# Two scatters pulled forward, four query loads moved to other buffers, and a DRAIN ahead of each store

## The chip, the cores and the metric

The kernel runs on one core of one Trainium2 chip. A core has five instruction queues that work at the same time: PE (matmuls), DVE (elementwise on vectors), ACT (activations), POOL (GpSimd) and SP (here it only issues DMAs). PE's weight loads are listed apart as PEld. The metric is the device time of one execution in microseconds (us), median of several runs.

## The reference, cut to what matters

Two stages follow each other. A linear attention gives 4608 rows of 512 numbers, and a mixture of experts sends each row through the one expert that its direction fits best:

```python
def phi(x):
    proj = np.einsum('bhsd,md->bhsm', x, omega)
    h = proj - np.sum(x * x, axis=-1, keepdims=True) / 2.0
    return np.exp(h - np.max(h, axis=-1, keepdims=True)) / np.sqrt(m)
q_p, k_p = phi(q * scale), phi(k * scale)
kv = np.einsum('bhsm,bhsd->bhmd', k_p, v)
out = einsum(q_p, kv) / (einsum(q_p, k_p.sum(2)) + 1e-6)      # 8 x 576 rows of 8 heads x 64
...
expert_idx = np.argmax(xn @ en.T / tau, axis=1)               # one of 8 experts for each row
for e in range(E):
    mask = expert_idx == e
    h = np.maximum(x[mask] @ w1[e], 0.0)                      # 512 -> 1024
    out[mask] = gate_w[mask, None] * (h @ w2[e])              # 1024 -> 512
```

## The kernel before, in words

**First stage: 36 tiles of 128 rows.** Queries and keys come as 36 tiles each. A loop over i (L711) handles key tile i and query tile iq = i - 7 together, so that i runs from 0 to 44: up to i = 6 there are only keys, from i = 36 on only queries. For a query tile the order on PE is: its projection (L362, 16 small matmuls), the transposes of the tile before (L449, 16), and the product with the finished key-value sums (L469, 32). ACT makes the exponentials (L375) and copies half of the transposes (L454), DVE makes the maxima (L366), the other copy (L456) and the normalised row tile xr (L482 to L488).

**Routing.** After each third query tile a generator (routed, L493) picks the experts of the three tiles, works out the place of each row in a table in memory (xs), sorted by expert, and POOL then writes each of the three tiles there with one indirect DMA, a scatter (L555). The generator is cut into nine steps. A list named plan (L837 to L844) says after which part of which iteration each step runs: (ends, k) is the end of iteration k, (mid, k, n) and (spare, k, n) are slots inside it. The last three steps are the three scatters. Three tiles are a group; there are 12, numbered from 0, so that the ninth is group 8, tiles 24 to 26, and its plan is made at i = 34. POOL runs its instructions in the order in which they are written.

**Queries and keys.** Each query tile (qt) goes through a ring of two buffers, as each key tile (kt) does through another. SP issues the load of query tile iq + 2 at the top of iteration i (loadq, L349; called at L713); a load waits until PE has done the projection that last read its buffer. The last key tile, 35, is read by PE in iteration 35. SP takes its loads in order: a load that waits holds those behind it.

**Beside the last iterations** the kernel already loads the weights of the most frequent expert (rf, L584), splits them into a high and a low part (L590 to L599; the low part on POOL), and starts on that expert's first two tiles of rows (first_steps, fs_x, fs_a, fs_o in the rows), among them a square root in 13 small POOL instructions (root, L138; rtt_p, rt_p in the rows).

**Second stage: 38 steps of 128 rows.** In each step PE does 24 matmuls with w1 (pb, L278) and 24 with w2 (po, L278); each takes 512 columns. POOL makes the low parts of the next weights in four pieces for w1 and four for w2 (L233) and between them stores the finished rows of an earlier step into the output with an indirect DMA (store, L307 to L315). The steps 0 and 1 are the two early tiles, the rest runs from t = 2 to 37; a further loop for more steps is not entered with these inputs.

Of the kernel before, what the change touches and what calls it, by code (L numbers as in the profile page):

```python
# [11 lines left out]
F32 = mybir.dt.float32  # L12
# [10 lines left out]
P = 128  # L23
# [6 lines left out]
NTILE = NSB * TPS  # L30
# [9 lines left out]
NPRE = 2  # L40
# [2 lines left out]
FILLS = {36: 1, 37: 1, 38: 1, 39: 1, 40: 1, 41: 1, 42: 1, 43: 2, 44: 4}  # L43
PADP = 8
ONACT = 5
PIECE = 256
SHIFTW = 16
BESIDE = 32
# [13 lines left out]
def attention_moe(ctx: ExitStack, tc: tile.TileContext, qT, kT, v1, omT, emb, tau, w1q, w2q, xs, out):  # L62
    nc = tc.nc
# [155 lines left out]
    def wsplit(wn, t, raw, dv, dp):  # L219
# [7 lines left out]
        else:  # L227
            ih = nc.vector.tensor_copy(at(h, dv), raw)  # L228
            ils = []
            piece = F if t is None or t >= NSTAT - 2 else PIECE  # L230
            for c in range(0, F, piece):
# [73 lines left out]
        return gp.tile([P, n], F32, name=f"{name}{t}", tag=name, bufs=2)  # L305

    def store(t, xg):  # L307
        w = nc.gpsimd.indirect_dma_start(
            out=out, out_offset=bass.IndirectOffsetOnAxis(ap=xg[:, PAY - 1 : PAY].bitcast(I32), axis=0),
            in_=xg[:, 0:DM], in_offset=None, bounds_check=N - 1, oob_is_err=False,  # L310
        )
        for o in outs:
            tc.declare_no_dep(w.ins, o.ins.name, reason="other tokens")
        outs.append(w)

    with ExitStack() as c1:
        p1 = c1.enter_context(tc.tile_pool(name="p1", bufs=2))
# [4 lines left out]
        kva, kvs, st = {}, {}, {}  # L322
# [25 lines left out]

        def loadq(i):  # L349
            if 0 <= i < NTILE:  # L350
                st["q", i] = p1.tile([P, 4, P], F32, name=f"qt{i}", tag="qt", bufs=2)
                nc.sync.dma_start(st["q", i], qT[i])


# [231 lines left out]
        def first_split(n):  # L586
            q, (_, h, l) = n // 2, W[("w1", "w2")[n % 2]]
            raw = st["rf", n]
            if n % 2 == 0 or n >= ONACT:
                nc.scalar.activation(h[:, 0, q, :], raw, AF.Copy)  # L590
# [10 lines left out]
        def first_steps():  # L601
# [16 lines left out]
            def down(t, cs, po):  # L618
                for c in cs:
                    computed("w2", t, products(po, pre_h[t], "w2", 0, [c], 0, c == 0, c == 7))  # L620
                    yield
                if c == 7:
                    scaled(po, xgp[t], total[:, t : t + 1])
                    store(t, xgp[t])
# [68 lines left out]
        early, spare, mid, ends, behind = {}, {}, {}, {}, []  # L693
# [16 lines left out]
        loop.enter_context(tc.manual_schedule(engines={ET.DVE, ET.Activation}))  # L710
        for i in range(NTILE + LAG + 2):  # L711
            iq = i - LAG
            loadq(iq + 2)  # L713
            ahead = i + (4 if i < 2 else 2)
            if i < 2 or i >= 4:
                load(ahead)
# [116 lines left out]
            if sums and done % G == G - 1:  # L833
                g = done // G
                steps = routed(g)
                if g == GPICK:
                    plan = [(ends, i), (mid, i + 1, 2), (mid, i + 1, 1), (spare, i + 2, 0), (mid, i + 2, 0)]  # L837
                    plan += [(mid, i + 3, 2), (mid, i + 3, 1)] + [(ends, i + 3 + k) for k in range(3)]
                elif i >= NTILE:
                    plan = [(ends, i)] * 3 + [(spare, i + 1, 0), (mid, i + 1, 0), (mid, i + 1, 1)]  # L840
                    plan += [(ends, i + 1 + k) for k in range(3)]
                else:
                    plan = [(ends, i), (mid, i + 1, 2), (mid, i + 1, 1), (spare, i + 2, 0), (mid, i + 2, 0)]
                    plan += [(mid, i + 3, 2)] + [(ends, i + 3 + k) for k in range(3)]  # L844
                for d, *key in plan:
                    (at(d, *key) if key[0] < NTILE + LAG + 2 else behind).append((next, steps, None))
            go(ends, i)
# [10 lines left out]
            if i in LOADS:  # L858
                n = LOADS.index(i)
# [16 lines left out]
        t = lambda n, w=E, dt=F32: once.tile([P, w], dt, name=n)  # L876
# [164 lines left out]
    with tc.manual_schedule(engines={ET.PE, ET.Activation, ET.DVE, ET.Pool, ET.SP}):  # L1041
        xt[NPRE] = pre_x[0]
        turn, ends = {}, NSTAT - 1
# [70 lines left out]
        for t in range(NPRE, NSTAT):  # L1114
# [15 lines left out]
            def ended():  # L1130

                for v in list(po):
                    scaled(po.pop(v), xg[v], gates[v])
                    store(v, xg[v])
# [13 lines left out]
            if t > SHIFT:  # L1148
                for v in list(po):
                    po.pop(v)  # L1150
                    store(v, xg[v])
                split("w2", u)
                if t == ends:
                    split("w1", t)
# [153 lines left out]
```

## Time and profile before

| | us |
|---|---|
| median of 3 runs (lowest, highest) | 659.11 (658.09, 659.37) |
| the profiled execution | 658.08 |
| its span, first to last instruction | 656.5 |
| PE busy | 629.6 |
| DVE busy | 496.5 |
| ACT busy | 430.8 |
| POOL busy | 424.7 |

A busy time is the time in which at least one instruction of that engine runs; the ends of matmuls are modelled. Times in the rows count from the start of the span. A row of a timeline is: start, duration, engine, line, operation, what is written and read, how many, and in brackets how long the engine had been idle and what ended that. "issue" stands where nothing that the profile shows was waited for, "remote" where what released the engine could not be found.

### The profile page before, as it was taken

What the parts mean: (1) busy time and instruction counts of PE and PEld (TensorE: products, weight loads), DVE (VectorE), ACT (ScalarE), POOL (GpSimd) and SP (SyncE); (2) the same over time, 40 slices, a digit from 0 to 9 for tenths busy, and PEclk for the clock granted to TensorE, in tenths of its full rate; (3) what the DMA queues carried; (4) which work ended last, traced back from release to release, by engine and by line L of the source; (5) the groups of instructions that cost most, each with busy time, mean ns of one, the idle gap of its engine ahead of it and who ended that gap; (6) DMA issues with size and microseconds to landing.
All of it is one profiled execution on the core that took longest, in us unless ns stands there. A gap on an engine that the chain in (4) does not pass through costs nothing.

```text
span 656.5 us, 19022 instructions
## 1 busy us (share of the span) xinstructions
PE 629.6 (96%) x6289; PEld 534.6 (81%) x6290; DVE 496.5 (76%) x926; ACT 430.8 (66%) x1102; POOL 424.7 (65%) x585
## 2 busy tenths in 40 slices
PE   9999999999998899999999999999999999999992
PEld 8899898889876788888888888888888888888871
DVE  5788888898978654686778786868787867787940
ACT  6899888888895425655666665666565656666420
POOL 2113343335986234668879797888878886798862
PEclk9999999999999999999999999999999999999996
DMA  7546666667943168859778788888787977787620
GB/s 263 182 149 194 191 193 206 196 198 267 327 139 131 50 195 306 258 148 251 211 223 212 222 212 224 211 221 222 203 232 210 244 200 196 224 219 214 172 85 35
DMA packets 142238, 131.92 MB, mean 201 GB/s; under 512 B 106742, under 2 KB 106870, under 8 KB 142144
## 3 DMA queue, kind: packets, MB, share of 16 engines
q1 hardware_dynamic: 135520, 109.70, 59.2%
q0 software_dynamic: 6480, 20.91, 9.1%
q8 instruction: 57, 0.93, 0.6%
q14 instruction: 37, 0.30, 0.1%
q10 hardware_dynamic: 144, 0.07, 0.0%
HBM read 83.78 MB, written 21.97 MB: 161 GB/s over the span
## 4 chain that ended last, share of the span: by engine, by line
PE 84%; ACT 5%; DVE 4%; issue 2%; POOL 2%; DMA 1%; SPq 0%; POOLq 0%; DVEq 0%; ACTq 0%
PE pb L278 30%; PE po L278 29%; PE pb L362 8%; PE nuu L469 4%; PE kva L393 4%; ACT ftq L375 2%; PE nuu L449 2%; ACT ftk L375 2%; PE fs_o L278 2%; PE fs_a L278 1%; PE nuu L393 1%; PE pb L260 1%; PE nuu L431 1%; DVE xr L488 1%; ACT qp L454 1%
## 5 line engine op out<-in xcount | busy, mean ns | idle before, releaser
L233 POOL TENSOR_TENSOR w1l<-raww,w1h 128x256 f32 (+1 forms) x130 | 123.2, 947 | 44.7 <-DVE w1h L228 37.1
L233 POOL TENSOR_TENSOR w2l<-raww,w2h 128x256 f32 (+1 forms) x130 | 144.2, 1110 | 11.9 <-DVE w2h L228 3.5
L278 PE MATMUL po<-w2h,hh 128*128 (+1 forms) x288 | 112.3, 390 | 0.4 <-POOL w2l L233 0.4
L278 PE MATMUL po<-w2h,hl 128*128 (+1 forms) x288 | 112.2, 390 | 0.0
L278 PE MATMUL po<-w2l,hh 128*128 (+1 forms) x288 | 112.1, 389 | 0.0
L278 PE MATMUL pb<-w1h,xh 128*128 (+1 forms) x280 | 109.5, 391 | 0.0
L278 PE MATMUL pb<-w1h,xl 128*128 (+1 forms) x280 | 109.3, 390 | 0.0
L278 PE MATMUL pb<-w1l,xh 128*128 (+1 forms) x280 | 109.0, 389 | 0.0
L1031 DVE COPY pl<-pb 128x512 uint16<-128x512 uint16 x68 | 46.7, 689 | 60.4 <-ACT pl L1027 60.3
L375 ACT ACTIVATE ftk<-pb,nmk 128x128 f32<-128x128 f32 x288 | 80.5, 457 | 4.9 <-DVE nmk L366 4.9
L375 ACT ACTIVATE ftq<-pb,nmq 128x128 f32<-128x128 f32 x288 | 80.4, 417 | 2.0 <-DVE nmq L366 1.3
L1027 ACT ACTIVATE pl<-pb 128x512 uint16<-128x512 uint16 x68 | 39.3, 582 | 60.3 <-DMA t<-pl 42.5
L1049 DVE COPY wd<-t 128x1024 uint16<-128x1024 uint16 x68 | 67.1, 989 | 1.3 <-DMA t<-pl 1.2
L1065 ACT ACTIVATE hh<-wd 128x1024 fp32r<-128x1024 f32 x34 | 36.1, 1063 | 46.9 <-DVE wd L1049 41.3
L278 PEld LDWEIGHTS po<-w2h,hh 128*128 128x128 f32 x288 | 54.0, 188 | 11.9 <-POOL w2l L233 0.8
L278 PEld LDWEIGHTS po<-w2h,hl 128*128 128x128 f32 x288 | 54.1, 188 | 11.5 <-DVE hl L1069 0.4
L278 PEld LDWEIGHTS po<-w2l,hh 128*128 128x128 f32 x288 | 54.1, 188 | 11.3
L278 PEld LDWEIGHTS pb<-w1h,xl 128*128 128x128 f32 x280 | 52.5, 188 | 11.6 <-DVE xl L1068 0.6
L278 PEld LDWEIGHTS pb<-w1l,xh 128*128 128x128 f32 x280 | 52.6, 188 | 10.8
L278 PEld LDWEIGHTS pb<-w1h,xh 128*128 128x128 f32 x280 | 52.6, 188 | 10.7
L1069 DVE SCALAR_TENSOR_TENSOR hl<-wd,hh 128x1024 fp32r<-128x1024 f32 x34 | 53.7, 1580 | 7.2 <-ACT hh L1065 6.8
L366 DVE TENSOR_REDUCE nmq<-pb 128x4 f32<-128x512 f32 x72 | 48.6, 683 | 7.3 <-PE pb L362 6.0
(333 smaller groups left out, 1229.4 us busy)
## 6 DMA issues: line engine op xcount, KB each, us to landing
raww<-w1q SPq DMA_DIRECT2D x38, 512.0 KB
raww<-w2q SPq DMA_DIRECT2D x38, 512.0 KB
kt<-kT SPq DMA_DIRECT2D x36, 256.0 KB
qt<-qT SPq DMA_DIRECT2D x36, 256.0 KB
xgp<-xs SPq DMA_DIRECT2D x20, 260.5 KB
xg<-xs SPq DMA_DIRECT2D x18, 260.5 KB
rf<-w1q SPq DMA_DIRECT2D x4, 512.0 KB
rf<-w2q SPq DMA_DIRECT2D x4, 512.0 KB
```

Source lines behind the costliest of these rows:

```text
L233: ils.append(nc.gpsimd.tensor_tensor(at(l, dp)[:, c], raw[:, c], at(h, dp)[:, c].bitcast(F32), op=ALU.subtract))
L278: done.append(nc.tensor.matmul(dst, x[:, c * P : (c + 1) * P], ws.rearrange("p o f -> p (o f)"), start=(begin and i == 0 and k == 0), stop ...
L362: nc.tensor.matmul(st["pj" + w, i, a][:, c, :], st[w, i][r, c, :], om[r, :], start=True, stop=True)
L366: nc.vector.tensor_reduce(nm, st["pj" + which, i, a], axis=AX.X, op=ALU.max, negate=True)
L375: nc.scalar.activation(ft[:, h, :], pj[:, h, :], AF.Exp, bias=nm[:, h : h + 1])
L393: nc.tensor.matmul(acc[c : c + 64, h, :], ft[:, h, c : c + 64], vt[:, 2 * h + a, :], start=begin and h == 0, stop=u == 4 + 4 * b and h == 3,)
L469: nc.tensor.matmul(pn[a][s * D : s * D + D, h, :], st["qp", i, s][:, 2 * h + a, :], kvs[sb, int(u > 4 - s)][:, 4 * a + h, :], start=True, ...
L1027: nc.scalar.activation(planes[1][:, o : o + 512], halved(src)[:, :, 1], AF.Copy)
L1031: nc.vector.tensor_copy(planes[0][:, o : o + 512], halved(src)[:, :, 0])
L1049: nc.vector.tensor_copy(to, src)
L1065: nc.scalar.activation(hh, wd[:, 0:F], AF.Relu)
L1069: nc.vector.scalar_tensor_tensor(hl, wd[:, 0:F], 0.0, hh.bitcast(F32), op0=ALU.max, op1=ALU.subtract)
```

## The change

Three things change.

- **Scatters.** For the plan made at i = 34 (group 8) the three scatters stood at the ends of iterations 37, 38 and 39. Now two stand at the end of iteration 37 and the third in a slot early in iteration 38.
- **Loads.** At i = 36 the loads of query tiles 31 and 32 are both written, at 37 that of 33, at 38 that of 34, at 39 that of 35, one iteration earlier than before each; tiles 32 and 33 go into the two buffers of the key tiles.
- **DRAIN.** Ahead of each store of a finished row tile into the output, step 1 excepted, POOL gets a DRAIN instruction: 37 of them.

```diff
+QLOADS = {36: (31, 32), 37: (33,), 38: (34,), 39: (35,)}
...
     def store(t, xg):
+        if t == 0 or t != "x" and t >= NPRE:
+            nc.gpsimd.drain()
         w = nc.gpsimd.indirect_dma_start(
...
         def loadq(i):
             if 0 <= i < NTILE:
-                st["q", i] = p1.tile([P, 4, P], F32, name=f"qt{i}", tag="qt", bufs=2)
+                st["q", i] = p1.tile([P, 4, P], F32, name=f"qt{i}", tag="kt" if i in QLOADS[NTILE][1:] + QLOADS[NTILE + 1] else "qt", bufs=2)
                 nc.sync.dma_start(st["q", i], qT[i])
...
-            loadq(iq + 2)
+            for n in QLOADS.get(i, () if i >= NTILE else (iq + 2,)):
+                loadq(n)
...
                     plan += [(mid, i + 3, 2)] + [(ends, i + 3 + k) for k in range(3)]
+                if NTILE - 3 < i < NTILE:
+                    plan[-3:] = [(ends, i + 3), (ends, i + 3), (mid, i + 4, 3)]
```

On POOL, iterations 37 to 39: xs is the table, xr24 to xr26 are the tiles of group 8 and xr27 that of the next, rf7 is the last piece of the early weights, rtt_p the first instruction of the square root. Before, the first scatter of the group and what follows, then the other two behind the square root:

```order
L555 DMA xs<-xr24_3774,posi8_4384 38016x576
L599 TENSOR_TENSOR w2l_140<-rf7_4209,w2h_139 128x256 x4
L477 COPY xr29_4459<-ids_118 128x1
L146 TENSOR_TENSOR rtt_p_4468<-n2p_4280,rt_p_4467 128x2
```

```order
L154 TENSOR_TENSOR rt_p_4467<-rt_p_4467,n2p_4280 128x2
L555 DMA xs<-xr25_3905,posi8_4384 38016x576
L516 COPY xr27_4179<-raw9_4491 128x8
L516 COPY xr28_4369<-raw9_4491 128x8
L516 COPY xr29_4459<-raw9_4491 128x8
L477 COPY xr30_4574<-ids_118 128x1
L555 DMA xs<-xr26_4044,posi8_4384 38016x576
L555 DMA xs<-xr27_4179,posi9_4592 38016x576
```

Now, the same places:

```order
L558 DMA xs<-xr24_3774,posi8_4386 38016x576
L558 DMA xs<-xr25_3905,posi8_4386 38016x576
L602 TENSOR_TENSOR w2l_140<-rf7_4211,w2h_139 128x256 x4
L558 DMA xs<-xr26_4044,posi8_4386 38016x576
L480 COPY xr29_4467<-ids_118 128x1
L147 TENSOR_TENSOR rtt_p_4476<-n2p_4282,rt_p_4475 128x2
```

```order
L155 TENSOR_TENSOR rt_p_4475<-rt_p_4475,n2p_4282 128x2
L519 COPY xr27_4179<-raw9_4496 128x8
L519 COPY xr28_4371<-raw9_4496 128x8
L519 COPY xr29_4467<-raw9_4496 128x8
L480 COPY xr30_4579<-ids_118 128x1
L558 DMA xs<-xr27_4179,posi9_4597 38016x576
```

The scatters of tiles 25 and 26 have moved from behind the square root to in front of it, one on either side of the last weight split.

On SP, the last loads of the first stage, before (qt29 to qt35 are the query tiles, rf7 the last early weights):

```order
L352 DMA qt29_3935<-qT 128x512
L584 ISA
L584 DMA rf7_4209<-w2q 128x1024
L352 DMA qt30_4072<-qT 128x512
L352 DMA qt31_4207<-qT 128x512
L352 DMA qt32_4304<-qT 128x512
L352 DMA qt33_4390<-qT 128x512
L352 DMA qt34_4502<-qT 128x512
L352 DMA qt35_4600<-qT 128x512
```

And now:

```order
L355 DMA qt29_3935<-qT 128x512
L587 ISA
L587 DMA rf7_4211<-w2q 128x1024
L355 DMA qt32_4209<-qT 128x512
L355 DMA qt30_4072<-qT 128x512
L355 DMA qt33_4306<-qT 128x512
L355 DMA qt31_4207<-qT 128x512
L355 DMA qt34_4395<-qT 128x512
L355 DMA qt35_4507<-qT 128x512
```

Tiles 32 and 33 have gone ahead of 30 and 31. PE, DVE and ACT keep their instructions in the same order.

## Rows read from the trace of the kernel before

**Rows 1.** The page's busy line: engine, busy us (share of the span), instructions.
```profile
PE 629.6 (96%) x6289; PEld 534.6 (81%) x6290; DVE 496.5 (76%) x926; ACT 430.8 (66%) x1102; POOL 424.7 (65%) x585
```

**Rows 2.** Stretches: length, busy us (instructions) of PE, PEld, DVE, ACT, POOL, clock, DMA share, GB/s.
```profile
212.50:215.90 3.40, 3.40 (x25) 2.64 (x27) 2.53 (x11) 1.95 (x8) 0.59 (x4) 0.51 0.02 5
300.00:350.00 50.00, 50.00 (x223) 41.40 (x222) 39.39 (x51) 30.40 (x56) 42.15 (x42) 1.00 0.82 221
```

**Rows 3.** The chain that ended last, 204 to 222: start, us, what.
```profile
204.97 1.18 PE nuu L469 x32
206.15 0.90 PE fs_a L278 x3
207.05 1.24 PE pb L362 x15
...
208.92 0.41 PE nuu L469 x8
...
212.39 1.42 PE fs_a L278 x3
213.81 2.01 PE pb L362 x16
```

**Rows 4.** ACT's timeline in the same stretch.
```profile
211.78 0.60 ACT L454 ACTIVATE qp<-pb 128x512 f32<-128x512 f32 x1 [3.63 <-remote]
```

**Rows 5.** POOL's timeline, iterations 37 to 43.
```profile
195.57 1.00 POOL L555 DMA_INDIRECT xs<-xr,posi  x1 [0.16 <-DVE nmq L366]
197.08 2.77 POOL L599 TENSOR_TENSOR w2l<-rf,w2h 128x256 fp32r<-128x256 f32 x4 [0.50 <-ACT w2h L590]
...
199.96 0.20 POOL L146 TENSOR_TENSOR rtt_p<-n2p,rt_p 128x2 f32<-128x2 f32 x1
...
204.05 1.03 POOL L555 DMA_INDIRECT xs<-xr,posi  x1 [0.53 <-issue]
...
207.14 0.99 POOL L555 DMA_INDIRECT xs<-xr,posi  x1 [0.30 <-issue]
...
209.82 0.98 POOL L555 DMA_INDIRECT xs<-xr,posi  x1 [0.16 <-POOL xr L477]
...
222.27 0.99 POOL L555 DMA_INDIRECT xs<-xr,posi  x1 [0.16 <-POOL xr L477]
```

**Rows 6.** PE's timeline, 150 to 240.
```profile
222.59 1.25 PE L469 MATMUL nuu<-kvs,qp 128*64 128x73 f32 x32
...
233.21 0.39 PE L278 MATMUL fs_o<-w2l,w2h 128*128 128x512 f32 x1
```

**Rows 7.** DMA queues, 208 to 212, then 212 to 216: packets, MB, share.
```profile
q0 software_dynamic: 253, 0.85, 57.1%
...
q8 instruction: 1, 0.02, 1.5%
```

**Rows 8.** SP's loads, then PE's waits, whole run: total us, times, longest.
```profile
178.68 0.34 SPq L584 DMA_DIRECT2D rf<-w2q  x1
179.12 25.64 SPq L352 DMA_DIRECT2D qt<-qT  x6
...
PE pb L362 <- DMA kt<-kT: 0.3, 1, 0.3
```

**Rows 9.** POOL's timeline in the second stage.
```profile
409.85 0.99 POOL L308 DMA_INDIRECT y<-xgp  x1 [0.16 <-issue]
...
431.91 1.28 POOL L308 DMA_INDIRECT y<-xg  x1 [0.15 <-DVE pl L1031]
433.22 4.08 POOL L233 TENSOR_TENSOR w2l<-raww,w2h 128x256 f32 x4
```

**Rows 10.** The chain that ended last, second stage.
```profile
440.56 5.44 PE po L278 x24
```

**Rows 11.** POOL's timeline at the end.
```profile
635.63 2.39 POOL L233 TENSOR_TENSOR w2l<-raww,w2h 128x1024 f32 x1 [3.46 <-DVE w2h L228]
...
645.17 0.99 POOL L308 DMA_INDIRECT y<-xgp  x1 [2.29 <-DVE xgp L1232]
```

## The prediction, on record before the result was known

> **What bounds the kernel now.** I read the busy line first, then the stretches, then the chain that ended last. PE is busy for 629.6 of 656.5 us [rows 1], so only PE's gaps, or a slower PE, can move the end. In the second stage there is no gap: in 300 to 350 PE is busy for all 50.00 us at clock 1.00 [rows 2], and the chain there is nothing but matmuls, 24 in 5.44 us [rows 10]. That stage, from about 258 to 631, can be made slower by this change but not faster. What can be won lies in the first stage and the turn to the second, before 258.
>
> The chain between 204 and 222 shows one place that is not like its neighbours. The 32 small matmuls of L469 take 1.18 us from 204.97 on; the next set begins at 208.92 and the step behind it only at 212.39, 3.47 us later, with pieces of "issue" between them [rows 3]. PE waits there for no engine and no DMA that the profile names. ACT, which needs only the transposes that PE had finished by 208.92, starts at 211.78 after 3.63 us of idling, released by "remote" [rows 4]: what PE sends out is late too, not only what it takes in. Behind this hole the granted clock is 0.51 from 212.5 to 215.9 [rows 2], the lower of PE's two levels (1.2 GHz instead of 2.4), and back at the full level afterwards.
>
> In just these microseconds POOL issues five scatters in a row: the first at 204.05, the third at 207.14, the last at 209.82 [rows 5]; their packets fill 57.1% of the DMA engines from 208 to 212 with no other queue beside them [rows 7]. They are the second and third scatter of group 8, held back behind the square root, and the three of group 9.
>
> **Scatters.** After the change two of the five are gone from this place. By POOL's rows: the second scatter follows the first at 195.57 + 1.00 + 0.30 (the gap ahead of the one at 207.14), so from 196.9 to 197.9. The split of w2l starts near 198.0 instead of 197.08, takes 2.77 and ends at 200.7. The third scatter then runs from about 201.2 to 202.2, with the 0.53 gap of the row at 204.05. The square root (199.96 to 203.5 before) ends near 206, and the copies and the first scatter of group 9 come at about 207.0, where 207.14 stood before [rows 5]. So group 9 stays where it was, with three scatters in place of five. What is delayed has cover: the split's result is first used at 233.21 [rows 6], 32 us later, and the root's reader on DVE comes in program order behind the matmuls of group 9's tiles. These moves cost nothing by themselves.
>
> What they are worth is whether the hole goes. A row of three scatters alone, group 10, has its second at 222.27; 32 matmuls of L469 start at 222.59 in the midst of it and take 1.25 us, undisturbed [rows 5, 6]. So I take it that three are harmless and five are not. If the hole goes, the gain is the sum of three differences on the chain: L469 3.47 - 1.18 = 2.29; the next three matmuls of L278 at the low clock 1.42 - 0.90 = 0.52; the projection 2.01 - 1.24 = 0.77 [rows 3]. That is 3.58 us. All work behind it hangs on PE's order, so the rest of the chain moves up whole. The lower end is the hole alone, 2.29, if the clock still falls; the upper end, with the weaker stretching of the tile before (1.24 for 15 matmuls) and the next transposes, I put at 4.4.
>
> **Loads.** SP issues its last six query loads between 179.12 and 204.8, each held by the projection that frees its buffer [rows 8]. Now tiles 32 and 33 don't wait for queries 30 and 31, and the last load goes out two tiles earlier, since it waits for the projection of tile 31 and no longer for that of tile 33. That wins nothing directly: in the whole run PE waited for a load once, 0.3 us, for a key tile [rows 8]; the last query tile was issued by 204.8 and used at 213.81 [rows 3]. The other side: tile 30 now stands behind tile 32 on SP, by one issue, while its own buffer was freed. The loads go out two tiles ahead of their use, as the last one shows with some 9 us, and of that one issue goes, 0.44 us from a start to the next [rows 8]. Cost nothing, at most those 0.44. SP has nothing else to issue here, so no queue behind it suffers. A side effect helps the scatters: the last load, just ahead of the five, is out of the way.
>
> **DRAIN.** 37 of them, on POOL only. Per second-stage step of 10.88 us (two blocks of 5.44) POOL is busy 42.15 / 50 x 10.88 = 9.17 and idle 1.71 [rows 2, 10]. Its w2 split ends at 437.30 and PE takes it at 440.56 [rows 9, 10]: 3.26 us in hand. The trace does not show a DRAIN's length. From below: a store right behind a split took 0.99 once and 1.28 another time [rows 9]; if a DRAIN takes out that difference it even saves POOL 0.3. From above: the longest thing that POOL runs here, one split of 2.39 [rows 11]. I take the lower rows, 0 to 0.3 per step, since the split ahead has ended 0.15 before the store starts [rows 9] and there is next to nothing to wait for. Behind the DRAIN stand the store and the w2 split, whose reader has the 3.26 us. At the end the split at 635.63 waits for DVE after 3.46 of idling, and the last store after 2.29 [rows 11]; a DRAIN in those pauses is free. Cost 0.
>
> The Trainium skill (GPSIMD Engine Reference, Instruction dispatch) says that a Pool instruction does not hold back the next: each of the eight cores goes on as soon as its own share is done. By that rule a DRAIN takes an overlap away; the rows that could show it are those two stores, and by them it is 0.3 us a step, inside POOL's 1.71, so the sum stays.
>
> **Sum.** The profiled execution took 658.08: 658.08 - 3.58 = 654.5. It was the fastest of what was timed; from the median of 659.11 the same gain leads to 655.5, which is my figure.
>
> **Rivals.**
> 1. *The hole belongs to PE's place and not to the scatters, or three suffice for it.* PE's instructions are the same and in the same order. For it: the one block of PE's instructions that is fetched near here comes at 212 to 216, right after the hole [rows 7], and I have no row in which the cause is seen. Against: dense small matmuls ran all through the first stage without such a hole. Time 659.1. The Trainium skill (Runtime: NRT & Kernel Launch, Instruction fetch mechanics) says that code is fetched in blocks of 256 instructions ahead of need, mostly hidden; by that rule the fetch is no cause, and the trace agrees in that the fetch comes after the hole's end and not in it.
> 2. *A second hole.* If scatters hurt wherever two are close together beside PE's small matmuls, the pair at 195.6 and 196.9, with the third at 201, makes a hole in iterations 38 to 39, and the three at 207 keep theirs. Price as above: 659.1 + 3.6 = 662.7. It decides once two scatters in flight suffice. Against it speaks the same undisturbed row at 222.59, where a second scatter had just begun.
> 3. *DRAIN as the bound.* If a DRAIN takes over 1.71 us, POOL sets the step. With 2.39: 34 steps x 0.68 = 23 us, 682. Nothing in the rows is that slow without cause.
>
> **How the numbers follow.** The hole goes: 0.52, at 655.5, own range 654.5 to 656.9. Nothing changes: 0.32, at 659.1. Second hole: 0.12. DRAIN: 0.04. A measurement of this kernel tells about 0.2% from no change, 1.3 us. So faster 0.52, same 0.32, slower 0.16. The range that leaves out the second hole, the DRAIN and a little below is 654.4 to 661.0.
>
> **What would show it.** Right: in iteration 41 the 32 matmuls of L469 take 1.2 us, the clock stays at 1.00 from 200 to 220, ACT's copy there is released by PE's transposes, and the second stage starts some 3.6 us earlier and keeps its 5.44. POOL shows scatters near 196.9 and 201, three near 207 to 210. Wrong: a piece of "issue" of over 1 us inside L469 again, there or in iterations 38 to 40; POOL's share near 100% with PE waiting for w1l or w2l; or a profile without the hole and an unchanged time, which would mean that the hole never cost the timed runs anything.

## The result, and the profile after

The changed kernel takes 667.23 us (median of 4 runs, 666.32 to 669.50), the kernel before 658.60 beside it (4 runs, 657.20 to 659.37): a ratio of 1.0139, 95% interval 1.0105 to 1.0172. I had forecast 655.5, between 654.4 and 661.0; it is 8.6 us slower than before and not 3.6 faster. The profiled execution took 667.99 us, its span is 666.1.

PE's timeline tells where the time went, when it is cut at four places: the first matmul of fs_o, the first of the run of equal blocks of 24 (299.0 before), PE's last matmul, and the end of the span.

| us | first stage | turn | steady | end | span |
|---|---|---|---|---|---|
| before | 233.0 | 66.0 | 344.9 | 12.7 | 656.5 |
| changed | 233.4 | 69.8 | 355.5 | 7.3 | 666.1 |

The first stage gained nothing, the turn lost 3.8, the steady stage 10.6, and the end gave back 5.4. I take them in this order. First the busy line, and the stretches of [rows 2] with two more:

```profile
PE 633.8 (95%) x6289; PEld 534.2 (80%) x6290; DVE 495.9 (74%) x926; ACT 430.8 (65%) x1102; POOL 427.0 (64%) x585
```

```profile
212.50:215.90 3.40, 2.98 (x42) 2.25 (x41) 3.27 (x9) 2.66 (x9) 0.00 (x0) 1.00 0.24 83
300.00:350.00 50.00, 50.00 (x224) 41.40 (x223) 36.10 (x49) 28.74 (x54) 40.71 (x41) 1.00 0.80 217
350.00:400.00 50.00, 48.37 (x212) 39.35 (x211) 38.87 (x51) 31.56 (x57) 42.10 (x40) 1.00 0.78 206
400.00:450.00 50.00, 48.59 (x213) 39.61 (x212) 37.63 (x52) 28.91 (x58) 40.76 (x41) 1.00 0.80 212
```

The busy line is no help: POOL's share falls by a point, since a DRAIN counts as no work. The stretches show it: the low clock at 212.5 is gone (1.00 for 0.51), but from 350 on PE has gaps of 1.4 to 1.6 us in 50.

**First stage.** The scatters moved as I had worked out (POOL's timeline, answering [rows 5]):

```profile
197.28 1.00 POOL L558 DMA_INDIRECT xs<-xr,posi  x1 [0.16 <-DVE nmq L369]
198.58 1.00 POOL L558 DMA_INDIRECT xs<-xr,posi  x1 [0.30 <-issue]
...
202.54 0.99 POOL L558 DMA_INDIRECT xs<-xr,posi  x1 [0.17 <-issue]
...
208.60 1.03 POOL L558 DMA_INDIRECT xs<-xr,posi  x1 [0.90 <-DVE nmq L369]
```

The hole did not go. The 32 matmuls around it, which took 3.54 us in all from 208.85 on, start at 211.31 now and take 2.22 us, with pauses at "issue" inside them as before (PE's timeline); undisturbed sets take 1.25 us. So 1.0 us of the 2.3 is left, beside three scatters, while the step behind them runs at the full clock:

```profile
211.31 0.67 PE L472 MATMUL nuu<-kvs,qp 128*64 128x73 f32 x13
212.15 0.39 PE L472 MATMUL nuu<-kvs,qp 128*64 128x73 f32 x5 [0.17 <-issue]
212.85 0.68 PE L472 MATMUL nuu<-kvs,qp 128*64 128x73 f32 x14 [0.30 <-issue]
```

And the chain in front of this place now runs over DVE, where before it was on PE:

```profile
203.89 0.56 issue
204.45 0.68 DVE nmq L369
205.12 0.61 DVE qp L459
...
207.50 1.18 PE nuu L472 x32
```

The stage ends at the same time. The two profiles hide a little here: the first set of 32 starts at 31.88 us after the change and at 30.10 before it, and kernels with nothing changed there have both values. Between the sets of query tiles 30 and 35, where the moves act, PE takes 21.2 us and took 22.4.

**Turn.** POOL's timeline from the last padding transfers on (xs<-w1l, issued by POOL as well) to the fourth store (store 3):

```profile
246.67 0.54 POOL L892 DMA_DIRECT2D xs<-w1l  x1 [0.51 <-issue]
255.54 1.04 POOL L311 DMA_INDIRECT y<-xgp  x1 [8.32 <-DVE hl L263]
256.88 1.00 POOL L311 DMA_INDIRECT y<-xgp  x1 [0.30 <-issue]
257.89 4.76 POOL L227 TENSOR_TENSOR w2l<-raww,w2h 128x1024 fp32r<-128x1024 f32 x2
...
287.96 0.99 POOL L311 DMA_INDIRECT y<-xgp  x1 [5.30 <-DVE xgp L286]
291.72 0.98 POOL L311 DMA_INDIRECT y<-xg  x1 [2.77 <-DVE xl L263]
```

The first store stands 8.32 us behind the last padding transfer, the fourth 2.77 behind the third; the second, which has no DRAIN, follows in 0.30. DVE is named as the releaser and had long been done: what POOL sits out is the DRAIN. The first one's record, in the row below, runs for 7.96 us; the padding's last packets land 5.7 us after its start. So a DRAIN waits for transfers of POOL's own that are still under way, which I had not thought of.

```profile
L310 POOLq DRAIN  x37: 917/927/7961, 246.7 to 657.7; - x37
```

**Steady stage.** Here nothing is under way when a DRAIN comes, and its median is 0.93 us. Two stores, to be held against those of [rows 9]:

```profile
430.48 1.37 POOL L311 DMA_INDIRECT y<-xg  x1 [0.94 <-DVE wd L1055]
431.89 4.65 POOL L234 TENSOR_TENSOR w2l<-raww,w2h 128x256 f32 x4
...
441.50 1.31 POOL L311 DMA_INDIRECT y<-xg  x1 [0.94 <-DVE pl L1037]
```

The gap ahead of a store is 0.94 in place of 0.15: 0.79 us in each step. It ends 0.15 us after the split, but only then does POOL's queue take up the store's own preparation, which had run beside the split before. The waits of 300 to 600 (total us, times, longest), PE's and POOL's, then SP's for the buffers:

```profile
POOL w1l L234 <- DVE w1h L229: 14.7, 11, 2.0
...
PEld pb L279 <- DVE xl L1074: 10.0, 10, 1.7
...
PE pb L279 <- DVE xl L1074: 5.8, 8, 1.3
```

```profile
SPq L182 <- DMA y<-xg: 9.1, 9, 1.2
SPq L182 <- DMA y<-xgp: 6.8, 5, 3.0
```

PE does not wait for the splits that I had watched (3.26 us in hand) but for xl, the rows of the coming steps. The chain shows how they become late, from a w1 split to the matmuls' operands:

```profile
518.62 0.67 issue
519.29 0.77 POOLq L310
...
521.01 4.29 DMA y<-xg
525.31 2.64 DMA xg<-xs
...
527.98 0.63 ACT pl L1033
528.61 0.52 ACT pl L1035
529.13 1.32 ACT wd L1057 x2
```

On this chain the DRAIN delays the store, the store's landing frees one of six row buffers, and the load of new rows into it waits for that; ACT and DVE turn them into operands behind it.

**End.** Behind PE's last matmul the program is 5.4 us shorter. The record of the program's own last DRAIN on POOL, before and after:

```profile
L1304 POOLq DRAIN  x3: 44/109/6694, 649.0 to 656.2; - x3
```

```profile
L1310 POOLq DRAIN  x3: 52/109/549, 664.2 to 665.8; - x3
```

The row of before stood in my trace, and I had written that no row shows a DRAIN's length. It is 6.69 us, with every transfer landed by 649.0. The Trainium skill (VectorE: DVE Perf Modes, "The DRAIN you can't avoid") calls the DRAINs that the runtime puts at a program's beginning and end a constant of some 12 ns on all five engines. Those of the rows stand on the kernel's own closing line (L1304), of which the page does not speak: on SP, ACT, DVE and PE the trace is near its figure (7 to 17 ns), on POOL it is 6694 ns, and the measurement decides.

### The profile page after: what moved, and what is told of

Read it like the earlier page. It is cut to its first block, busy times and chain, and to the rows that moved or that the text cites. A ratio compares the mean times of both kernels' runs of the same rounds, so it can differ in the third digit from the quotient of the medians.

```text
span 666.1 us, 19061 instructions
## 1 busy us (share of the span) xinstructions
PE 633.8 (95%) x6289; PEld 534.2 (80%) x6290; DVE 495.9 (74%) x926; ACT 430.8 (65%) x1102; POOL 427.0 (64%) x585
## 4 chain that ended last, share of the span: by engine, by line
PE 31%; DMA 18%; issue 14%; ACT 14%; DVE 11%; POOL 5%; POOLq 4%; SPq 1%; DVEq 0%; ACTq 0%
PE pb L365 9%; PE nuu L472 5%; PE kva L396 5%; DMA t<-pl 4%; ACT wd L1057 4%; ACT pl L1033 3%; PE pb L279 3%; DMA xg<-xs 3%; DMA y<-xg 3%; DMA xgp<-xs 3%; DMA y<-xgp 3%; PE po L279 2%; POOLq L310 2%; PE nuu L452 2%; DVE wd L1055 2%
## 5 line engine op out<-in xcount | busy, mean ns | idle before, releaser
L1055 DVE COPY wd<-t 128x1024 uint16<-128x1024 uint16 x68 | 60.3, 887 | 1.8 <-DMA t<-pl 1.8
L279 PEld LDWEIGHTS pb<-w1l,xh 128*128 128x128 f32 x280 | 52.6, 188 | 10.8
```

Source lines behind the costliest of these rows:

```text
L279: done.append(nc.tensor.matmul(dst, x[:, c * P : (c + 1) * P], ws.rearrange("p o f -> p (o f)"), start=(begin and i == 0 and k == 0), stop ...
L1055: nc.vector.tensor_copy(to, src)
```

## The experiments

Each ratio is to runs of the kernel before in the same group (650.9 to 653.0 us in three groups, 660.1 to 660.7 in two); the stages are cut as above, in the kernel's own profile, and kernels with nothing changed in the steady stage differ there by up to 3 us from one profile to the next. Where the groups' 8 us come from is not settled; nearly all of it lies in the first stage, about half of it between the sets of query tiles 30 and 35 (18.4 to 19.1 us in the profiles of the groups around 651 us, 21.2 to 23.9 in those around 660). The number of the chip does not decide it: the record has number 10 for a group at 651.8 and for one at 660.1.

| kernel | ratio (95% interval) | first | turn | steady | end |
|---|---|---|---|---|---|
| before_again | (one run) | 228.0 | 66.1 | 345.1 | 12.7 |
| drain_only | 1.0152 (1.0117 to 1.0188) | 226.4 | 74.3 | 357.5 | 7.3 |
| drains_third | 1.0134 (1.0109 to 1.0159) | 231.6 | 70.8 | 355.7 | 7.3 |
| no_drain | 1.0012 (0.9985 to 1.0039) | 227.9 | 66.9 | 346.5 | 12.7 |
| no_drain_again | 1.0016 (0.9998 to 1.0035) | 225.2 | 66.1 | 344.5 | 12.7 |
| moves_third | 0.9995 (0.9975 to 1.0014) | 235.4 | 66.0 | 347.6 | 12.7 |
| scatters_only | 1.0012 (0.9990 to 1.0035) | 226.4 | 66.0 | 344.5 | 12.7 |
| loads_only | 1.0002 (0.9982 to 1.0022) | 226.6 | 66.8 | 345.8 | 12.7 |
| drain_turn | 0.9975 (0.9953 to 0.9997) | 225.9 | 71.8 | 346.9 | 8.3 |
| delay_ahead | 1.0406 (1.0380 to 1.0432) | 225.2 | 66.7 | 370.8 | 14.6 |
| delay_behind | 1.0171 (1.0146 to 1.0195) | 227.4 | 66.8 | 358.5 | 14.1 |
| store_piece | 1.0065 (1.0040 to 1.0090) | 233.5 | 66.0 | 347.7 | 12.7 |
| drain_early | 1.0060 (1.0036 to 1.0083) | 233.0 | 71.6 | 349.5 | 7.3 |
| drain_in_wait | 0.9928 (0.9898 to 0.9958) | 233.3 | 67.8 | 345.6 | 5.5 |
| drain_two | 0.9888 (0.9857 to 0.9920) | 235.8 | 66.4 | 345.9 | 5.5 |
| drain_two_again | 0.9891 (0.9877 to 0.9906) | 225.4 | 66.3 | 344.5 | 5.5 |
| two_and_moves | 0.9906 (0.9890 to 0.9922) | 226.1 | 66.0 | 346.1 | 5.5 |

### Which part of the change it is

drain_only and drains_third are the kernel before with the DRAINs; no_drain, no_drain_again and moves_third are the changed kernel without them:

```diff
     def store(t, xg):
+        if t == 0 or t != "x" and t >= NPRE:
+            nc.gpsimd.drain()
```

scatters_only and loads_only have one of the other two parts alone.

> The kernel before with the 37 DRAINs alone; scatters and loads as before. Theory A (the DRAIN is the whole loss): in the trace of the changed kernel PE falls behind the kernel before by 3.8 us between 218 and 297 and by 10.8 between 297 and 604, and the stretch behind POOL's last store is 7.2 us shorter (2.9 instead of 10.1). With the first stage unchanged that gives 658.6 + 3.8 + 10.8 - 5.4 = 667.8, between 666.5 and 669.5, and POOL's final DRAIN takes 0.55 us and not 6.69. Rival B (the moved scatters or loads make the loss, for instance by other load times all through): 658.6 within 1.3.

> The changed kernel without its DRAINs: scatters and loads as changed. Theory A: the second stage is as before (50.00 of 50 us of PE busy in 300 to 350, the last stretch 10.1 us), and only the first stage differs: the hole of 3.58 us at 208.9 to 212.4 is gone, but a smaller one has come at 196.6 (2.73 for 32 matmuls instead of 1.2, 1.5 lost): 658.6 - 3.58 + 1.5 = 656.5, between 655.0 and 658.6. Rival B: about 667.

> The kernel before with group 8's scatters moved, nothing else. Theory A: the moved scatters carry all of the first stage's gain: 656.5, the same as with the loads, within 0.6. If the loads have a part in it (the first stage's hole came with a load beside the scatters, or the later pairs of loads meet the scatters), it differs from the kernel with both by more than 0.6. If the hole had nothing to do with the scatters: 658.6.

> The kernel before with the six query loads moved and two of them in the keys' buffers, nothing else. By my prediction nothing: 658.6 within 0.5. If the early loads take the DMA engines from the scatters or the values, or the keys' buffers make a load wait, 1 us or more slower, with a wait of PE for a query or key tile near 180 to 215.

The DRAINs are the whole loss: 1.5% alone, 1.4% in the changed kernel. Two of the three profiles with all DRAINs agree on where the loss lies (turn 3.8 and 4.8 us, steady 10.6 and 10.8); drain_only shows more (8.3 and 12.6), since the granted clock fell there to 0.51: from 260.3 to 267.2, around a gap of PE of 4.56 us, and from 420.7 to 424.2, behind gaps of 0.5 and 1.2 us. PE was busy for 4.95 and 3.50 us of these, so by estimate the lower clock makes up 2.4 and 1.7 us of the difference.

Scatters and loads are worth nothing measurable, and this disproved my 656.5 for them. (The smaller hole at 196.6 in that sum was none: these 32 matmuls take 1.25 us in PE's timeline, and the chain's 2.73 runs on to where DVE was released.) So I looked for the hole itself:

> The kernel before once more, for one profile. If the hole of 3.47 us in front of the step behind L469's 32 matmuls (208.92 to 212.39) belongs to the five scatters, it stands here again, at the same matmuls. If it was an event of that one execution, these 32 matmuls take 1.18 us here too, and my gain of 3.58 us was never in the timed runs. The last DRAIN of the program takes 6.69 us either way.

It was not there: all 94 matmuls of 208 to 212.5 run at clock 1.00, with the same five scatters beside them (203.8 to 209.5). That left the question whether the gain exists where the hole does:

> The changed kernel without its DRAINs, once more. In the profiles of the first run of the kernel before and of three of its variants, the five scatters stand beside a hole at 208 to 212 and the low clock behind it; in those of two other groups of runs the same five stand there without a hole, and the moves of scatters and loads were worth nothing. If the hole costs the timed runs of the chips on which it appears, and these runs are on such a one, the moves are worth 2 to 4 us here: -0.3% to -0.6%. If the profile of this group shows the first stage without a hole, or a hole costs nothing, 0 within 0.3%.

> The changed kernel without its DRAINs, a third time. Where the kernel before takes 658 to 661 us, its profiles have the hole in the first stage; where it takes 650 to 653, they have none and the moves were worth nothing (twice). If the kernel before takes about 659 here and the hole is what the moves take away: 2 to 4 us less. If it takes about 651: 0 within 0.3% a third time, and the question stays open.

> The kernel before with the 37 DRAINs alone, beside the moves alone on the same chip: +1.5% as in its first run. The changed kernel's +1.4% less this is what the moves are worth beside the DRAINs, 0 or a gain up to 0.4%.

no_drain_again fell into a group where the kernel before takes 651, moves_third into one where it takes 660, as in the first profile. There the moves gained nothing either (0.9995). The kept profiles show that the hole goes with the group. The 32 matmuls of query tile 32 take 3.16 to 4.11 us in the six profiles around 660 us that have the scatters in their old place (drains_third, in the same group as moves_third: 3.53), 2.22 and 2.26 in the two with moved scatters (the changed kernel and moves_third), and 1.25 in all eleven around 651 us, moved or not. So where the hole is, the moves shrink it but do not take it away. The granted clock falls to its lower level behind it in five of the six, in neither of the two. Two stretches of moves_third (columns as in [rows 2]) show where the gain is lost:

```profile
200.00:208.00 8.00, 6.32 (x97) 4.86 (x99) 6.26 (x20) 5.10 (x18) 6.80 (x17) 1.00 0.28 102
...
212.50:216.00 3.50, 2.98 (x54) 2.49 (x52) 2.06 (x5) 1.15 (x5) 1.56 (x3) 1.00 0.51 186
```

PE idles for 1.7 us just ahead of the place, where it is busy throughout in drains_third (8.00 of 8.00 us); the 0.5 in the second stretch, at the full clock, are the pauses that are left of the hole. The chain from 201.8 to 207.6 is DVE there: routing and maxima one after the other, as in the changed kernel. From the set of query tile 30 to that of tile 35 moves_third takes 21.4 us and drains_third 21.6, the changed kernel 21.2 and the kernel before 22.4: 0.2 and 1.2 us less, where I had counted 3.58, and the timed runs do not resolve that much. (The 3.8 us by which moves_third's first stage is longer than drains_third's lie ahead of this place: 2.0 are there at the first set of 32, behind 3.4 us at a granted clock of 0.5 from 7.4 on, and 1.7 between query tiles 24 and 30.) As I read it, part of the hole was slack that PE had run up on DVE; where it shrinks, PE waits for DVE instead. What makes the pauses, and why only in some groups, no run shows.

### What a DRAIN waits for

> The kernel before with one DRAIN alone, ahead of the first store. Theory A1 (a DRAIN waits for every transfer that POOL has issued and pays for each of them): it takes about 8 us as in the kernel with all 37 (7.96 and 8.50), the first two stores come 8 us late, the w2 split behind them too, PE loses 2 to 5 us between 250 and 300, and the program's last DRAIN, with 38 transfers left of 74, takes about 38 / 74 x 6.69 = 3.4 us: +0 to +2 us in sum. Theory A2 (the end's DRAIN has a fixed price): the last stays at 6.69, and the sum is +2 to +5.

```diff
+        if t == 0:
+            nc.gpsimd.drain()
```

A1 holds for the DRAINs. The turn pays 5.7 us (by estimate 1.7 of it for 3.5 us of matmuls at a granted clock of 0.51 from 261.7 on, behind PE's pause), and the program's last DRAIN falls from 6.69 to 3.17. POOL has issued 81 transfers in the whole program (36 scatters, 7 of padding, 38 stores), and 38 of them are left here: 0.083 us each both times. In sum that is nearly even (0.9975, 1.6 us less, where A1 had 0 to 2 more).

### Lateness of the store, or POOL's time

> The kernel before, no DRAIN, and three small MEMSETs into a scratch tile (about 0.8 us together, what a DRAIN adds) ahead of each store of steps 6 to 37. Theory T1 (the later store is what costs, since the load into the buffer that it frees goes out later): PE loses about what it loses with the DRAINs between 300 and 604, 8 to 14 us, with waits of PE for xl. Theory T2 (POOL's lost time is what costs, wherever it stands): the same 8 to 14 here. If only what a DRAIN waits for costs and not its length: 0 within 2.

> The same three MEMSETs behind each store instead of ahead of it: POOL does the same work in a step, but the store goes out when it did before. T1: no loss, 0 within 2 us, PE busy for 50.0 of 50 us. T2: the same 8 to 14 us as ahead of the store.

```diff
+    def paused(t):
+        if t != "x" and t > SHIFT:
+            for n in (240, 240, 96):
+                nc.gpsimd.memset(pause[0][:, 0:n], 0.0)
     def store(t, xg):
+        paused(t)                  # delay_behind: the call stands after the store
```

The three MEMSETs took 0.9 us, and ahead of a store 1.3 with the preparation behind them. The steady stage lost 25.9 us with them ahead, more than either theory had, and 13.6 with them behind, against 0 by T1: T1 alone is wrong. Next each suspect by itself:

> The kernel before, no DRAIN; each store of the second stage stands behind the first of the four pieces of the w2 split, not ahead of it. POOL's work in a step is the same, the store goes out about 1.0 us later. T1 (the store's lateness costs, by the reload of the buffer that it frees): a loss like the DRAIN's or more, 8 to 20 us. T2 (POOL's time costs, wherever it stands): 0 within 2 us.

> The kernel before with the 37 DRAINs, and in the second stage each DRAIN and store stand ahead of the last of the four pieces of the w1 split: the store goes out about when it did before (1.0 earlier, 0.8 later), POOL pays for the DRAIN as before. T1: the loss of the steady stage (11 to 12 us) goes, what stays is the turn's 4 to 8 less the 5.4 to 7 of the end: 0 within 3 us. T2: the same +9.9 as with the DRAINs alone.

> The kernel before with a DRAIN ahead of store 2 and 31 DRAINs ahead of the w1 splits of steps 6 to 36, where POOL waits for DVE's w1h in most steps (23 of 27, 1.36 us on average), and none ahead of a store. T1: the stores are late only in the steps without that wait, the steady stage loses 0 to 3 us; the end's DRAIN falls from 6.69 to about 0.55, 6 us less: -3 to -6 in sum. T2: POOL's lost time counts in the steps where it doesn't wait and little in the others, 3 to 6 us, and -3 to 0 in sum.

```diff
             if t > SHIFT:
-                for v in list(po):
-                    po.pop(v)
-                    store(v, xg[v])
-                split("w2", u)
+                split("w2", u, {0: stores})      # store_piece: the loop, after piece 0 of 4
...
-                split("w1", t if t > NPRE else 0)
+                split("w1", t if t > NPRE else 0, {2: stores})   # drain_early: after piece 2
...
+            if SHIFT < t < ends:                 # drain_in_wait, and one ahead of store 2
+                nc.gpsimd.drain()
             if t not in (NPRE + 1, ends):
                 split("w1", t if t > NPRE else 0)
```

A later store with the same work on POOL costs 0.65%, 4.3 us (2.8 of it in its profile's steady stage, which is within what profiles differ by). The DRAIN with a store that is on time costs 4.6 there, both together 10.8 and 12.6. The same DRAIN in the wait for w1h costs 0.7, so T2, by which it would cost wherever it stands, is wrong too. The whole times say the same: store_piece (+4.3 us) and drain_early (+4.0) lie between what the two theories had, drain_in_wait (-4.8) where T1 had it. A step of drain_in_wait looks like before, 0.16 ahead of the store and the 0.68 of waiting still there:

```profile
401.53 1.28 POOL L310 DMA_INDIRECT y<-xgp  x1 [0.16 <-issue]
402.84 4.07 POOL L233 TENSOR_TENSOR w2l<-raww,w2h 128x256 f32 x4
407.59 3.52 POOL L233 TENSOR_TENSOR w1l<-raww,w1h 128x256 f32 x4 [0.68 <-DVE w1h L228]
```

What fits them all, an inference and not a test: the piece of a step that counts is the one from DVE's w1h over w1 split and store to the end of the w2 split. Spread over 34 steps, 0.79 us of DRAIN in it costs 0.32 to 0.37 with the store late and 0.14 with it on time, 1.3 us ahead of the store 0.76, 1.0 behind it 0.40. That is an estimate of 0.4 to 0.7 us to spare per step, where I had counted 1.71. By which of two ways the rest comes back, the store's landing or the weight loads that SP holds until a split has freed their buffer, no run separates.

### A version that beats both

> The kernel before with two DRAINs alone: ahead of store 2, where POOL idles at the turn, and ahead of the last but one w2 split, where it idles for 3.46 us. If a DRAIN pays for each transfer issued since the last one, 0.09 us each (6.69 / 74): the first takes about 4 us for 45 transfers, the second about 3 for 33, both beside the idle time, and the program's last about 0.55 for 3. That is 6 us less at the end, with at most 1 us lost at the two places: -4 to -6 us. If the end's DRAIN doesn't count transfers: 0.

> The kernel before with the two DRAINs alone (ahead of store 2 and of the last but one w2 split), once more, beside the next. By the count of transfers (0.084 us each in its first profile) -7 us again, -0.9% to -1.3%.

> The changed kernel with those two DRAINs in place of its 37: scatters and loads moved as in the change. If the moves are worth nothing: as drain_two, -7 us. If the moves keep their 2 to 4 us where the hole is: -9 to -11 us.

```diff
     def store(t, xg):
+        if t == 2:
+            nc.gpsimd.drain()
...
+        nc.gpsimd.drain()
         split("w2", ends - 1)
```

```profile
L309 POOLq DRAIN  x1: 4556/4556/4556, 282.4 to 282.4; - x1
...
L1225 POOLq DRAIN  x1: 5690/5690/5690, 633.6 to 633.6; - x1
...
L1307 POOLq DRAIN  x3: 46/109/598, 651.8 to 653.3; - x3
```

```profile
288.41 0.99 POOL L310 DMA_INDIRECT y<-xgp  x1 [5.26 <-DVE xgp L285]
...
639.95 2.38 POOL L233 TENSOR_TENSOR w2l<-raww,w2h 128x1024 f32 x1 [3.42 <-DVE w2h L228]
```

Two DRAINs in pauses that POOL has anyway take 7.4 and 7.1 us off (0.9888 and 0.9891): the end falls from 12.7 to 5.5 and nothing else moves. POOL's last piece of work before them ends at 283.15 and 636.53 (the splits at 279.98 and 634.15); from there they take 3.78 us for 45 transfers and 2.78 for 33, 0.084 each, inside pauses as long as before (3.42 here, 3.46 in [rows 11]). With the moves it is 1.0 us slower than without, within the two intervals.

## Why the prediction was wrong

- **DRAIN, cost 0: the step that failed.** It cost 1.34% and 1.52% alone, 8.8 and 9.9 us. Three things in it were wrong. "There is next to nothing to wait for" looked at the split alone and not at POOL's transfers, nor at the store's preparation, which the DRAIN puts behind the split: 0.79 us and not 0 to 0.3. "Inside POOL's 1.71" took all idle time of an average step for slack; POOL's pauses lie ahead of w1h, and the DRAIN stands behind it. "Whose reader has the 3.26 us" looked at the split behind the DRAIN and not at the store's own reader, the load into the freed buffer.
- **The upper end and rival 3.** My bound of 2.39 was not passed in the steady stage (0.79), but it was at the turn (8 us at the first store), and POOL never became the bound in the way I priced. The loss came at less than half the 1.71 from which I had let it decide.
- **Scatters, -3.58.** The moves on POOL came where I had put them and the low clock went, but the gain did not come. Two steps failed. "Three are harmless and five are not": beside three the 32 matmuls still lose 1.0 us (2.22 against 1.25), and the second profile of the kernel before has the five and no hole. "The rest of the chain moves up whole": DVE was close behind PE. My rival 1 (the hole belongs to PE's place, or three suffice for it; the time unchanged) was right for this part; which of its two halves holds stays open.
- **Loads, 0.** Right: 1.0002.
- **The second stage "can be made slower but not faster".** Right, and so is its start: PE is busy for 50.00 us of 300 to 350 after the change too. The loss begins later, as I take it when the steps' slack is used up.
- **The end.** I had no term for it. The changed kernel won 5.4 us there, which the 37 DRAINs had paid for many times over.

## What to carry to other kernels

Before an instruction is put ahead of another, look at what the queue prepares for that other one beside running work, and at who waits for what it releases, a buffer too: an engine's idle time is slack only where the new instruction stands in front of the wait. A program whose GpSimd issues many transfers pays for each of them in a DRAIN at its end, and a few DRAINs in pauses that GpSimd has anyway take that price off the end. A gap on the engine that bounds a stage is worth something only if the next engine in the chain is not right behind it; whether it is there in other executions too, and whether it is gone after the change, is read at the same matmuls.

## What the runs showed of the hardware

- A DRAIN on POOL costs 0.083 to 0.084 us for each transfer that POOL has issued since the last one, though all have landed: 6.69 us for 81, 3.78 for 45, 3.17 for 38, 2.78 for 33. With only one or three, whose packets were still landing when it began, it took 0.55 and 0.60.
- It waits for POOL's transfers still under way: 2.77 us between two stores in a row, 0.30 without it.
- With one landed transfer it ends 0.15 us after POOL's work, and the next store starts 0.79 us later than without it.
- On SP, ACT, DVE and PE the DRAINs of the program's end take 7 to 17 ns in the same profile.
- In all eight profiles of the groups around 660 us PE pauses inside the same 32 matmuls, which take 1.0 to 2.9 us longer by it; in the eleven of the groups around 651 us it does not, with the same scatters beside them.
